# Packing the value projection of a segmented attention kernel, and running its last two blocks as one group

## The chip, the cores and the metric

The kernel runs on one core of a Trainium2 chip. The metric is the device time of one execution in microseconds (us). Engines are named as in the profile: PE is TensorE (matmuls), PEld its weight loads, DVE is VectorE, ACT is ScalarE, POOL is GpSimd, and SP issues most of the DMAs. Line numbers such as L419 are lines of the kernel whose profile is shown.

## The reference

Two branches are added to `x`. Branch B is an MLP mixer, which the change does not touch. Branch A is attention over 64 segments of 32 rows. A segment sees its own rows and some memory rows, which come from the segment before.

```python
# 2048 rows, Dm = 1024, 32 heads of 128, M = 8 memory rows, segments of 32 rows
for s in range(n_seg):
    h = concat([mem, xs])                       # 8 memory rows + 32 rows of the segment
    q, k, v = h @ Wq, h @ Wk, h @ Wv            # each 1024 -> 32 x 128
    p = softmax(mask(q k^T * scale))
    o = (p v) @ Wo
    mem = o[:M]; outs.append(o[M:])
return x + concat(outs) + B(layernorm(x))
```

## The kernel before

The recurrence would run the segments one after another. The kernel guesses all memory rows first (`speculate`), computes all segments in parallel and verifies the guess at the end; a fallback exists and does not run here. The guess gives the eight memory rows that a later segment sees the same value, so one row stands for all eight (the mask adds log2 of 8 to its score), and such a segment takes 33 columns of the transposed activations `hT`. Three segments make a tile of 99 columns (106 for the first, 33 for the last), and four tiles make a block. There are six blocks, and the last one has only two tiles. The weights of a head group (four heads) are three tiles of 1 MB, loaded anew in each block.

```python
for b in range(6):
    hTb = hpool.tile([P, KT, NBMAX], BF16, tag="hTb")       # 403, 396 or 132 columns used
    nc.sync.dma_start(hTb[:, :, lb:nb], hT_d[:, :, c0 + lb:c1])
    ...                                  # DVE writes the guessed memory columns (reps) into hTb
    for hg in range(8):
        wq, wk, wv = ...                 # three loads of 1 MB on SP, four buffers
        for hh in range(4):              # Q; the same for K
            ps = apsum.tile([P, 512], F32, tag="mm")        # two PSUM buffers
            for k in range(KT):
                nc.tensor.matmul(ps[:, :nb], wq[:, k, hh*P:(hh+1)*P], hTb[:, k, :nb], ...)
            nc.scalar.mul(QT[:, hh, :nb], ps[:, :nb], QSCALE)
        for ti, (tok, T, msk) in enumerate(btiles):         # V, one matmul group per tile
            ps = apsum.tile([P, 512], F32, tag="mm")
            for k in range(KT):
                nc.tensor.matmul(ps[:T, :], hTb[:, k, l0:l0+T], wv[:, k, :], ...)
            nc.scalar.copy(V[:T, ti, :], ps[:T, :])
        for ti, (tok, T, msk) in enumerate(btiles):         # attention
            ...  # S = QT^T KT (psS); softmax on DVE and ACT: sm, mx, sm, e, ss, rs, Pn
            ...  # transposes (psT), PT; O = V^T PT (psO), oS on ACT
        ...      # DVE sorts oS into oX (rows) and oT_m (memory rows)
    out_proj(oX, b, ns, mid=(verify() if b == 5 else None))
```

The order of instructions on each engine is fixed when the program is built. Each engine, and SP as the issuer of DMAs, then works through its own list in that order and waits where data or a buffer is missing (below, DVE stands 8.47 us at one such place, with other work behind it).

Of the kernel before, what the change touches and what calls it, by code (L numbers as in the profile page):

```python
# [13 lines left out]
BF16 = mybir.dt.bfloat16  # L14
# [7 lines left out]
P = 128  # L22
# [40 lines left out]
def kernel(  # L63
# [30 lines left out]
    hT_d = tc.dram_tile([P, KT, TH], BF16, name="hT_scratch")  # L94

# [19 lines left out]
    mask40 = const_tile("c_mask40", np.tile(_seg_mask(1, True), (1, 8)))  # L115
    G = cpool.tile([NQ, D], F32)
    ZT = cpool.tile([P, KT, NQ], BF16)
    M0T = cpool.tile([P, KT, M], BF16)
# [10 lines left out]
    def speculate(psum, wpool, spool):  # L129
# [5 lines left out]
        nc.vector.tensor_copy(M0T[:], ps9[:, :, 0:M])  # L135
# [26 lines left out]
        for k0 in (0, 4):  # L162
            ps = psum.tile([P, 4, NQ], F32, tag="tr")
            for k in range(4):
                nc.tensor.matmul(ps[:, k, :], Gb[:, (k0 + k) * P:(k0 + k + 1) * P], ident[:NQ, :NQ], start=True, stop=True)
            nc.vector.tensor_copy(ZT[:, k0:k0 + 4, :], ps[:])
        nc.vector.tensor_reduce(gthr[:], G[:], axis=AX.X, op=ALU.max, apply_absolute_value=True)
        nc.vector.tensor_scalar(gthr[:], gthr[:], TOL, None, op0=ALU.mult)


    actx = ctx.enter_context(ExitStack())
    with ExitStack() as bctx:
# [117 lines left out]
        with ExitStack() as p3:  # L290
# [7 lines left out]
            for tb in range(4):  # L298
# [5 lines left out]
                if tb == 3:  # L304
                    rctx.close()
                    wpool = actx.enter_context(tc.tile_pool(name="aw", bufs=4, side="right"))
                    spool = actx.enter_context(tc.tile_pool(name="aspec", bufs=1, side="right"))
                    hpool = actx.enter_context(tc.tile_pool(name="ah", bufs=2, side="right"))
                    qkv = actx.enter_context(tc.tile_pool(name="aqkv", bufs=2, side="right"))
                    speculate(psum, wpool, spool)  # L310
# [17 lines left out]
    if True:  # L328
# [7 lines left out]
        def out_proj(oX, b, ns, mid=None):  # L336
            for gl in range(ns // 4):
                Gi = 3 * b + gl
                Rt = iop.tile([P, D], F32, tag="Rt")
                nc.sync.dma_start(Rt[:], R_v[:, Gi, :])  # L340
                ot = iop.tile([P, D], BF16, tag="ot")
                for ch in range(2):
                    ps = apsum.tile([P, 512], F32, tag="mm")
                    for h in range(H):
                        nc.tensor.matmul(ps[:], oX[:, h, gl * P:(gl + 1) * P], wo_sb[:, h, ch * 512:(ch + 1) * 512], start=(h == 0), stop=(h == H - 1))  # L345
                    if DEBUG_A:
                        nc.vector.tensor_copy(ot[:, ch * 512:(ch + 1) * 512], ps[:])
                    else:
                        nc.vector.tensor_tensor(ot[:, ch * 512:(ch + 1) * 512], ps[:], Rt[:, ch * 512:(ch + 1) * 512], op=ALU.add)
                    if mid is not None and ch == 0:  # L350
                        mid()
                nc.sync.dma_start(out_v[:, Gi, :], ot[:])

        def verify():
            Dm = iop.tile([NQ, D], F32, tag="Rt")
            for ch in range(2):
                ps = apsum.tile([P, 512], F32, tag="mm")
                for h in range(H):
                    nc.tensor.matmul(ps[:NQ, :], oT_m[:, h, :], wo_sb[:, h, ch * 512:(ch + 1) * 512], start=(h == 0), stop=(h == H - 1))
                nc.vector.tensor_tensor(Dm[:, ch * 512:(ch + 1) * 512], ps[:NQ, :], G[:, ch * 512:(ch + 1) * 512], op=ALU.subtract)  # L360
            dmax = smp.tile([NQ, 1], F32, tag="dmax")
            nc.vector.tensor_reduce(dmax[:], Dm[:], axis=AX.X, op=ALU.max, apply_absolute_value=True)
# [5 lines left out]
            def count():  # L368
                psc = apsum.tile([P, 512], F32, tag="mm")
# [4 lines left out]
        for b in range(6):  # L374
# [8 lines left out]
            if b == 0:  # L383
                nc.vector.tensor_copy(reps[:, :, 1:ns], ZT[:, :, 7:6 + ns])
                nc.vector.tensor_copy(hTb[:, :, 0:M], M0T[:])
            else:
                nc.vector.tensor_copy(reps, ZT[:, :, 12 * b + 6:12 * b + 6 + ns])
            oX = abig.tile([P, H, 384], BF16, tag="oX")
            btiles = tiles[4 * b:4 * b + 4]
            for hg in range(8):  # L390
                cs_ = slice(hg * 512, (hg + 1) * 512)
                hs_ = slice(hg * 4, (hg + 1) * 4)
# [6 lines left out]
                if b == 0 and 1 <= hg < 5:  # L399
                    nc.sync.dma_start(wo_sb[:, (hg - 1) * 8:hg * 8, :], Wo_v[:, (hg - 1) * 8:hg * 8, :])  # L400
                QT = qkv.tile([P, 4, NBMAX], BF16, tag="QT")
                KTt = qkv.tile([P, 4, NBMAX], BF16, tag="KT")
                V = qkv.tile([P, 4, 512], BF16, tag="V")
                oS = qkv.tile([P, 4, NBMAX], BF16, tag="oS")
                for hh in range(4):
                    ps = apsum.tile([P, 512], F32, tag="mm")
                    for k in range(KT):
                        nc.tensor.matmul(ps[:, :nb], wq[:, k, hh * P:(hh + 1) * P], hTb[:, k, :nb], start=(k == 0), stop=(k == KT - 1))  # L408
                    nc.scalar.mul(QT[:, hh, :nb], ps[:, :nb], QSCALE)  # L409
                for hh in range(4):  # L410
                    ps = apsum.tile([P, 512], F32, tag="mm")
                    for k in range(KT):
                        nc.tensor.matmul(ps[:, :nb], wk[:, k, hh * P:(hh + 1) * P], hTb[:, k, :nb], start=(k == 0), stop=(k == KT - 1))  # L413
                    nc.scalar.copy(KTt[:, hh, :nb], ps[:, :nb])  # L414
                for ti, (tok, T, msk) in enumerate(btiles):
                    l0 = tok - c0
                    ps = apsum.tile([P, 512], F32, tag="mm")
                    for k in range(KT):
                        nc.tensor.matmul(ps[:T, :], hTb[:, k, l0:l0 + T], wv[:, k, :], start=(k == 0), stop=(k == KT - 1))  # L419
                    nc.scalar.copy(V[:T, ti, :], ps[:T, :])  # L420
                for ti, (tok, T, msk) in enumerate(btiles):
                    l0 = tok - c0
                    psS = apsum.tile([P, 512], F32, tag="S", bufs=2)
                    S3 = psS[:T, :4 * T].rearrange("p (h k) -> p h k", h=4)
                    for hh in range(4):
                        nc.tensor.matmul(S3[:, hh, :], QT[:, hh, l0:l0 + T], KTt[:, hh, l0:l0 + T], start=True, stop=True)  # L426
                    sm = smp.tile([P, 4, 106], F32, tag="sm")
                    nc.vector.tensor_tensor(sm[:T, :, :T], S3, msk[:].unsqueeze(1).to_broadcast((T, 4, T)), op=ALU.add)  # L428
                    mx = smp.tile([P, 4], F32, tag="mx")
                    nc.vector.tensor_reduce(mx[:T, :], sm[:T, :, :T], axis=AX.X, op=ALU.max)  # L430
                    nc.vector.tensor_tensor(sm[:T, :, :T], sm[:T, :, :T], mx[:T, :].unsqueeze(2).to_broadcast((T, 4, T)), op=ALU.subtract)  # L431
                    e = smp.tile([P, 4, 106], F32, tag="e")
                    nc.scalar.activation(e[:T, :, :T], sm[:T, :, :T], ACTF.Exp, scale=LN2)  # L433
                    ss = smp.tile([P, 4], F32, tag="ss")
                    nc.vector.tensor_reduce(ss[:T, :], e[:T, :, :T], axis=AX.X, op=ALU.add)  # L435
                    rs = smp.tile([P, 4], F32, tag="rs")
                    nc.vector.reciprocal(rs[:T, :], ss[:T, :])  # L437
                    Pn = smp.tile([P, 4, 106], BF16, tag="Pn")
                    nc.vector.tensor_tensor(Pn[:T, :, :T], e[:T, :, :T], rs[:T, :].unsqueeze(2).to_broadcast((T, 4, T)), op=ALU.mult)  # L439
                    psT = apsum.tile([P, 512], F32, tag="T", bufs=1)  # L440
                    T3 = psT[:T, :4 * T].rearrange("p (h k) -> p h k", h=4)
                    for hh in range(4):
                        nc.tensor.matmul(T3[:, hh, :], Pn[:T, hh, :T], ident[:T, :T], start=True, stop=True)  # L443
                    PT = smp.tile([P, 4, 106], BF16, tag="PT")
                    nc.scalar.copy(PT[:T, :, :T], T3)  # L445
                    psO = apsum.tile([P, 512], F32, tag="O", bufs=2)
                    O3 = psO[:, :4 * T].rearrange("p (h k) -> p h k", h=4)
                    for hh in range(4):
                        nc.tensor.matmul(O3[:, hh, :], V[:T, ti, hh * P:(hh + 1) * P], PT[:T, hh, :T], start=True, stop=True)  # L449
                    nc.scalar.copy(oS[:, :, l0:l0 + T], O3)  # L450
                o4 = oS[:, :, lb:lb + 33 * ns].rearrange("p h (j i) -> p h j i", i=33)
                nc.vector.tensor_copy(oX[:, hs_, 0:32 * ns].rearrange("p h (j i) -> p h j i", i=32), o4[:, :, :, 1:33])  # L452
                nc.vector.tensor_copy(oT_m[:, hs_, 7 + 12 * b:7 + 12 * b + ns], o4[:, :, :, 0])
                if b == 0:
                    nc.vector.tensor_copy(oT_m[:, hs_, 0:7], oS[:, :, 0:7])
            out_proj(oX, b, ns, mid=(verify() if b == 5 else None))
# [3 lines left out]
    with tc.If(cond > 0):  # L460
        with ExitStack() as fctx:
# [5 lines left out]
            nc.sync.dma_start(wo_sb[:], Wo_v)  # L467
            hseg = fbig.tile([P, KT, L], BF16)
# [112 lines left out]
```

## Time and profile before

| | before |
|---|---|
| time | 1754.67 us median of 4 runs |
| PE busy | 97% of the span |
| attention part (block 0 to the end) | 586 to 1754.5 us |
| head group of blocks 1 to 4 | 21.1 us |
| head group of block 5 (scores to scores in the timeline) | 9.79 us |

Here are lines of the page of the kernel before: the span, busy time by engine (with share and instruction count), the granted clock in 40 slices (9 is full), and the groups of V (L419) and K (L413; Q, in L408, is like it). A group has busy time and mean ns of one instruction after the bar, then PE's idle time in front of it.

```profile
span 1754.5 us, 25780 instructions
PE 1707.1 (97%) x10705; PEld 923.9 (53%) x10705; DVE 642.4 (37%) x1515; ACT 669.0 (38%) x1347; POOL 90.9 (5%) x117
...
PEclk9999999999999999999999999999999999999999
...
L419 PE MATMUL ps<-wv,hTb 128*99 128x512 bf16 (+2 forms) x1408 | 315.4, 379 | 0.0
L413 PE MATMUL ps<-hTb,wk 128*128 128x396 bf16 (+2 forms) x1536 | 264.8, 313 | 1.7 <-ACT QT L409 1.7
```

PE is nearly always busy and hardly waits. A record of a V matmul lasts 379 ns, but the matmuls start 216 ns apart, so the records overlap. The real pace is read from the chain of the work that ended last (start, us, engine, output, line, count). These lines of it are from block 2:

```profile
1008.65 5.37 PE ps L408 x32
1014.03 5.37 PE ps L413 x32
1019.40 6.91 PE ps L419 x32
...
1040.51 6.91 PE ps L419 x32
```

A group of 32 V matmuls takes 6.91 us, 216 ns each, and the next V group starts 21.11 us later. So V is a third of a head group. It costs that much although its stationary operand has only 99 of 128 columns.

The windows view gives busy time by engine in each stretch, then clock, DMA share and GB/s. The stretches are block 0, block 2, block 5 and the tail.

```profile
core 0: us, PE busy (x) PEld busy (x) DVE busy (x) ACT busy (x) POOL busy (x), PEclk, DMA share, GB/s
586.14:797.44 211.30, 210.05 (x1345) 118.85 (x1345) 94.54 (x222) 94.17 (x193) 0.53 (x1) 1.00 0.54 179
1008.65:1219.67 211.02, 209.06 (x1346) 118.49 (x1344) 93.52 (x215) 92.24 (x192) 0.00 (x0) 1.00 0.43 135
...
1641.68:1718.82 77.14, 74.94 (x818) 51.31 (x816) 29.82 (x100) 39.49 (x122) 0.00 (x0) 1.00 0.89 283
1718.82:1754.50 35.68, 29.34 (x148) 14.00 (x145) 8.39 (x22) 2.33 (x7) 0.00 (x0) 0.97 0.03 9
```

Block 5 stands out with a DMA share of 0.89: it loads the same 24 MB of weights as any block and has a third of the work.

### The profile page before, as it was taken

What the parts mean: (1) busy time and instruction counts of PE and PEld (TensorE: products, weight loads), DVE (VectorE), ACT (ScalarE), POOL (GpSimd) and SP (SyncE); (2) the same over time, 40 slices, a digit from 0 to 9 for tenths busy, and PEclk for the clock granted to TensorE, in tenths of its full rate; (3) what the DMA queues carried; (4) which work ended last, traced back from release to release, by engine and by line L of the source; (5) the groups of instructions that cost most, each with busy time, mean ns of one, the idle gap of its engine ahead of it and who ended that gap; (6) DMA issues with size and microseconds to landing.
All of it is one profiled execution on the core that took longest, in us unless ns stands there. A gap on an engine that the chain in (4) does not pass through costs nothing.

```text
span 1754.5 us, 25780 instructions
## 1 busy us (share of the span) xinstructions
PE 1707.1 (97%) x10705; PEld 923.9 (53%) x10705; DVE 642.4 (37%) x1515; ACT 669.0 (38%) x1347; POOL 90.9 (5%) x117
## 2 busy tenths in 40 slices
PE   5999999999999999999999999999999999999998
PEld 3544444444445555545555455554555555555564
DVE  7447010000002255532555335551455505554242
ACT  6635302021120255513555145551555415553251
POOL 4222010110101000000000000000000000000000
PEclk9999999999999999999999999999999999999999
DMA  9454421121239874434444254451444434443590
GB/s 370 188 171 166 168 84 37 60 61 31 90 116 374 290 261 149 145 103 135 148 145 146 77 162 145 145 163 65 158 144 148 123 102 145 147 155 101 175 328 10
DMA packets 200793, 260.07 MB, mean 148 GB/s; under 512 B 6541, under 2 KB 167352, under 8 KB 200672
## 3 DMA queue, kind: packets, MB, share of 16 engines
q1 hardware_dynamic: 193472, 232.95, 41.3%
q0 software_dynamic: 7200, 25.44, 3.7%
q8 instruction: 85, 1.39, 0.3%
q14 instruction: 36, 0.29, 0.0%
HBM read 228.87 MB, written 29.49 MB: 147 GB/s over the span
## 4 chain that ended last, share of the span: by engine, by line
PE 77%; DVE 8%; ACT 5%; DMA 5%; issue 3%; POOL 0%; SPq 0%; DVEq 0%; ACTq 0%; POOLq 0%
PE ps L419 17%; PE ps L302 11%; PE ps L345 10%; PE ps L322 10%; PE ps L413 9%; PE ps L408 8%; PE psT L443 3%; PE psO L449 2%; PE psS L426 2%; DVE Pn L439 2%; DVE ss L435 2%; ACT e L433 2%; DMA xn_scratch<-xn 1%; DMA wv<-in_A_Wv_dram 1%; DMA hTb<-hT_scratch 1%
## 5 line engine op out<-in xcount | busy, mean ns | idle before, releaser
L419 PE MATMUL ps<-wv,hTb 128*99 128x512 bf16 (+2 forms) x1408 | 315.4, 379 | 0.0
L413 PE MATMUL ps<-hTb,wk 128*128 128x396 bf16 (+2 forms) x1536 | 264.8, 313 | 1.7 <-ACT QT L409 1.7
L408 PE MATMUL ps<-hTb,wq 128*128 128x396 bf16 (+2 forms) x1536 | 261.7, 314 | 1.8 <-DVE Ro L323 0.8
L419 PEld LDWEIGHTS <-hTb 128*99 128x99 bf16 (+2 forms) x1408 | 173.2, 124 | 124.6 <-issue 3.2
L345 PE MATMUL ps<-wo_sb,oX 128*128 128x512 bf16 x1024 | 229.6, 379 | 0.7 <-DVE flag_i L371 0.7
L409 ACT ACTIVATE QT<-ps 128x396 bf16<-128x396 f32 (+2 forms) x192 | 88.8, 463 | 346.2 <-PE ps L408 345.4
L322 PE MATMUL ps<-w_sb,h3T 128*128 128x512 bf16 x896 | 197.1, 379 | 0.0
L302 PE MATMUL ps<-xn3T,w_sb 128*128 128x512 bf16 x896 | 194.4, 379 | 0.0
L428 DVE TENSOR_TENSOR sm<-psS,c_mask_reg_sb 99x396 f32<-99x396 f32 x160 | 87.5, 564 | 290.6 <-PE psS L426 290.6
L420 ACT CAST V<-ps 99x512 bf16<-99x512 f32 (+2 forms) x176 | 103.1, 586 | 202.7 <-PE ps L419 202.7
L408 PEld LDWEIGHTS <-wq 128*128 128x128 bf16 x1536 | 133.8, 98 | 73.5 <-issue 2.4
L413 PEld LDWEIGHTS <-wk 128*128 128x128 bf16 x1536 | 133.3, 98 | 71.2 <-issue 2.6
L303 ACT ACTIVATE h3T<-ps 128x512 bf16<-128x512 f32 x112 | 66.7, 597 | 268.2 <-PE ps L302 268.2
L345 PEld LDWEIGHTS <-oX 128*128 128x128 bf16 x1024 | 97.7, 98 | 111.7 <-DVE oX L452 1.9
L302 PEld LDWEIGHTS <-w_sb 128*128 128x128 bf16 x896 | 87.6, 98 | 105.2
L322 PEld LDWEIGHTS <-h3T 128*128 128x128 bf16 x896 | 86.9, 98 | 103.0
L323 DVE TENSOR_TENSOR Ro<-ps,R 128x512 f32<-128x512 f32 x32 | 22.1, 691 | 296.5 <-PE ps L322 296.4
L445 ACT CAST PT<-psT 99x396 bf16<-99x396 f32 (+2 forms) x176 | 86.2, 490 | 59.2 <-PE psT L443 51.5
L414 ACT CAST KTt<-ps 128x396 bf16<-128x396 f32 (+2 forms) x192 | 87.5, 456 | 53.8 <-PE ps L413 52.5
L435 DVE TENSOR_REDUCE ss<-e 99x4 f32<-99x396 f32 (+2 forms) x176 | 94.7, 546 | 19.4 <-ACT e L433 19.3
L439 DVE TENSOR_TENSOR Pn<-e,rs 99x396 bf16<-99x396 f32 (+2 forms) x176 | 97.5, 558 | 8.1 <-DVE rs L437 0.5
L433 ACT ACTIVATE e<-sm 99x396 f32<-99x396 f32 (+2 forms) x176 | 90.1, 530 | 18.7 <-DVE sm L431 12.7
(101 smaller groups left out, 1317.1 us busy)
## 6 DMA issues: line engine op xcount, KB each, us to landing
wv<-in_A_Wv_dram SPq DMA_DIRECT2D x56, 1024.0 KB, 5.5
wq<-in_A_Wq_dram SPq DMA_DIRECT2D x48, 1024.0 KB, 5.5
wk<-in_A_Wk_dram SPq DMA_DIRECT2D x48, 1024.0 KB, 5.5
xt<-in_A_x_dram SPq DMA_DIRECT2D x32, 256.0 KB, 3.1
R_scratch<-x POOLq DMA_DIRECT2D x16, 512.0 KB, 3.8
R<-R_scratch SPq DMA_DIRECT2D x16, 512.0 KB, 4.1
R_scratch<-Ro POOLq DMA_DIRECT2D x16, 512.0 KB, 5.0
wo<-in_A_Wo_dram SPq DMA_DIRECT2D x8, 1024.0 KB, 9.4
```

Source lines behind the costliest of these rows:

```text
L302: nc.tensor.matmul(ps[:], w3_sb[:, k, f * P:(f + 1) * P], xn3T[:, k, tb * 512:(tb + 1) * 512], start=(k == 0), stop=(k == KT - 1))
L322: nc.tensor.matmul(ps[:], h3T[:, f, j * P:(j + 1) * P], w4_sb[:, f, ch * 512:(ch + 1) * 512], start=(f == 0), stop=(f == FT - 1))
L345: nc.tensor.matmul(ps[:], oX[:, h, gl * P:(gl + 1) * P], wo_sb[:, h, ch * 512:(ch + 1) * 512], start=(h == 0), stop=(h == H - 1))
L408: nc.tensor.matmul(ps[:, :nb], wq[:, k, hh * P:(hh + 1) * P], hTb[:, k, :nb], start=(k == 0), stop=(k == KT - 1))
L409: nc.scalar.mul(QT[:, hh, :nb], ps[:, :nb], QSCALE)
L413: nc.tensor.matmul(ps[:, :nb], wk[:, k, hh * P:(hh + 1) * P], hTb[:, k, :nb], start=(k == 0), stop=(k == KT - 1))
L414: nc.scalar.copy(KTt[:, hh, :nb], ps[:, :nb])
L419: nc.tensor.matmul(ps[:T, :], hTb[:, k, l0:l0 + T], wv[:, k, :], start=(k == 0), stop=(k == KT - 1))
L420: nc.scalar.copy(V[:T, ti, :], ps[:T, :])
L433: nc.scalar.activation(e[:T, :, :T], sm[:T, :, :T], ACTF.Exp, scale=LN2)
L435: nc.vector.tensor_reduce(ss[:T, :], e[:T, :, :T], axis=AX.X, op=ALU.add)
L439: nc.vector.tensor_tensor(Pn[:T, :, :T], e[:T, :, :T], rs[:T, :].unsqueeze(2).to_broadcast((T, 4, T)), op=ALU.mult)
```

## The change

The intent is to project V from tiles of 128 full rows. The 32 real rows of each segment are packed into `xTb`, so 12 segments need three row tiles in place of four. All 71 memory rows are projected once per head group, in block 0, and kept in DRAM. V is still needed in the order of the attention tiles, so small DMAs copy the packed rows, 32 at a time, to their places. Blocks 4 and 5 become one group that loads its weights once. The projections get a third PSUM buffer, `oS` has one buffer, the output projection works on half-width tiles, and its weights `Wo` come in eight loads, one per head group of block 0, in place of four.

```diff
+Vr_d = tc.dram_tile([NQ, H * DH], BF16, name="Vmem_scratch")
-ZT, M0T                                   # memory columns
+MZ = cpool.tile([P, KT, NQ + 1], BF16)    # both in one tile
 ...
+xTb = xvp.tile([P, KT, 32 * ns], BF16, tag="xTb" + sfx, bufs=1)
+nc.vector.tensor_copy(xTb[...], hTb[... columns 1 to 32 of each 33 ...])
 ...
-for ti, (tok, T, msk) in enumerate(btiles):
-    ps = apsum.tile([P, 512], F32, tag="mm")
-    for k in range(KT):
-        nc.tensor.matmul(ps[:T, :], hTb[:, k, l0:l0 + T], wv[:, k, :], ...)
-    nc.scalar.copy(V[:T, ti, :], ps[:T, :])
+for m in range(ns // 4):
+    ps = apsum.tile([P, 512], F32, tag="mm", bufs=3)
+    for k in range(KT):
+        nc.tensor.matmul(ps[:], xTb[:, k, m * P:(m + 1) * P], wv[:, k, :], ...)
+    nc.scalar.copy(Vp[:, m, :], ps[:])
+if b == 0:                                 # the memory rows of all segments
+    for k in range(KT):
+        nc.tensor.matmul(ps[:NQ, :], MZ[:, k, 0:NQ], wv[:, k, :], ...)
+    nc.vector.tensor_copy(vr[:], ps[:NQ, :])
+    nc.gpsimd.dma_start(Vr_d[:, cs_], vr[:])
+for sl in range(ns):                       # 12 copies (4 in block 5)
+    nc.sync.dma_start(V[r0:r0 + SEG, ti, :], Vp[SEG * (sl % 4):SEG * (sl % 4 + 1), sl // 4, :])
+... memory rows: block 0 from vr on POOL, other blocks from Vr_d on SP
 ...
-for b in range(6):
+for group in ((0,), (1,), (2,), (3,), (4, 5)):   # Q of all, K of all, V of all, attention of all
 ... (half-width output tiles, oS with one buffer, Wo in eight loads, a mask loaded in the fallback only: cut)
```

## The prediction

> **What bounds the kernel now.** TensorE. The page has PE busy 97% of the 1754.5 us span, clock row 9 throughout; DVE 37%, ACT 38%. PE's waits add up to some 35 us, mostly in the first stage; under 6 us in the attention blocks (586 us to the end). The timeline of blocks 1 to 4 shows a head group every 21.1 to 21.3 us: 5.37 us each for 32 matmuls of Q and of K (168 ns per 396 columns), 6.91 us for 32 of V (216 ns per 512 columns, from the chain), about 3.6 us for 48 small attention matmuls. The Trainium skill, "TensorE: Matmul & The Clock Gate", section "Back-to-back issue gap", gives N/2.4 + 2.5 ns (216 ns at N=512), without a term for the stationary columns; the trace agrees: V with 99, 106 or 33 stationary columns costs the same (379 to 380 ns records, 216 ns apart).
>
> Block 5 (1642.6 to 1719.0) takes 9.79 us per head group with 3 MB of weights; the windows view shows its DMA near saturation (up to 338 GB/s).
>
> **Removed.** V is projected from rows packed 128 at a time, without memory rows. Blocks 0 to 4: 4 row tiles to 3; block 5: 2 to 1; one extra tile in block 0 does all memory rows. V matmuls go from 1408 to 1088: 320 x 216 ns = 69 us, all on PE's chain: nothing in block 0, 13.8 us in each other block. Fewer evictions on ACT are worth nothing.
>
> **Merging blocks 4 and 5** loads weights once: 24 MB less. Without it block 5 would have become DMA-bound and lost its V gain. Block 5's attention gets more projection work to hide behind: I estimate 7.6 us per head group (2 x 2.1 Q and K, 1.7 V, 1.8 attention) in place of 9.8: 17 us, of which 13.8 is V, so 3 us extra. Tail: about 1 us.
>
> **Added.** 12 copies of 32 KB per head group (4 in block 5) plus the memory rows, SBUF to SBUF, between V's eviction and its use. A DMA issue occupies SP 0.37 us in this trace: about 5 us of SP per 19.5 us. The first use of V (psO) comes 6.6 us after V's last matmul, later tiles by 11 us. Copies may queue behind a 1 MB weight load (5.5 us); that mostly fits. Block 0 adds a serial tail of POOL-issued copies (0.55 us issue each, some 4 us to land), close to 6.6 us. Packing xTb costs DVE a few us per block, hidden. A V tile now depends on several DMAs: more semaphore waits on PE. I charge 0.1 to 0.2 us per head group, up to 1 us in block 0: 5 to 10 us in all. One oS buffer, and both Q/K buffers taken in the merged group, should not stop PE: scores are consumed early.
>
> **Prediction.** 1754.7 - 69 - 4 + 7 = about 1688 us; range 1670 to 1712. Faster by over 2%: 0.93; within 2%: 0.06; slower: 0.01.
>
> **What would show it.** V: 1024 + 64 matmuls, same 379 ns; head group in blocks 1 to 3 about 19.5 us, in block 0 still 21, merged about 27; PE above 95%; weight traffic down 24 MB; small copies landing in 2 to 7 us. Waits of psO on DMA into V under 10 us in total; tens of us would mean late copies.
>
> **What would make it wrong.** V copies stuck behind weight loads, or SP blocked behind a V copy so weights come late; the instruction order placing psO too early; the merged group starved at its last head group; block 0's POOL copies stalling each head group by several us.

## The result, and the profile after

The changed kernel takes 1681.21 us, median of 8 runs (1679.27 to 1683.68), against 1755.83 us for the kernel before in the same rounds. The ratio is 0.9576, with a 95% interval of 0.9566 to 0.9585. A ratio is the mean time of one kernel's fast runs over that of the other's of the same rounds, so it is not quite the ratio of the medians.

These lines of the page after answer to those of before.

```profile
span 1680.2 us, 26399 instructions
PE 1638.0 (97%) x10385; PEld 857.9 (51%) x10385; DVE 650.8 (39%) x1531; ACT 637.6 (38%) x1299; POOL 114.6 (7%) x164
...
L414 PE MATMUL ps<-wv,xTb 128*128 128x512 bf16 x1024 | 227.7, 379 | 0.0
```

The memory rows of block 0 are in a small group, shown by the list of groups by shape:

```profile
L419 PE MATMUL ps<-wv,MZ 128*71 128x512 bf16 x64 | 15.1, 379 | 0.0
```

V went from 1408 to 1024 + 64 matmuls of the same 379 ns, and PE is still 97% busy. By the two pages HBM reads fell from 228.87 to 204.11 MB, as forecast for one block's weights. The chain after, in block 2 and in the merged group (Q and K now share line L402):

```profile
998.36 10.75 PE ps L402 x64
1009.11 5.18 PE ps L414 x24
...
1028.55 5.18 PE ps L414 x24
...
1393.08 14.45 PE ps L402 x128
1407.53 6.91 PE ps L414 x32
...
1434.10 6.91 PE ps L414 x32
```

A head group takes 19.44 us in block 2 (1009.11 to 1028.55); 1.73 us fewer of V would make 19.4. In the merged group the interval between V groups is 26.57 us here and 26.7 us between the later ones (1434.10 to 1460.79). The windows view after, with the same columns, shows block 0, block 2, the merged group and the tail:

```profile
586.83:801.14 214.31, 211.76 (x1345) 112.95 (x1345) 101.19 (x231) 89.98 (x185) 24.83 (x49) 1.00 0.60 191
998.36:1195.58 197.22, 195.82 (x1281) 105.11 (x1280) 94.76 (x216) 87.58 (x184) 0.00 (x0) 1.00 0.52 161
1393.08:1600.95 207.87, 206.11 (x1785) 127.60 (x1783) 105.14 (x281) 113.08 (x285) 0.00 (x0) 1.00 0.40 122
1600.95:1680.20 79.25, 74.28 (x394) 35.23 (x392) 23.71 (x56) 8.20 (x19) 0.00 (x0) 0.98 0.15 46
```

The 74.3 us between the two profiles, by stage:

| stage | before | after | difference | 216 ns x V matmuls |
|---|---|---|---|---|
| before block 0 | 586.14 | 586.83 | +0.7 | 0 |
| block 0 | 211.30 | 214.31 | +3.0 | 0 |
| blocks 1 to 3 | 633.13 | 591.94 | -41.2 | -41.5 |
| blocks 4, 5 and tail | 323.93 | 287.12 | -36.8 | -27.6 |

So in blocks 1 to 3 the copies cost nothing that can be seen, in block 0 something costs 3 us, and the merged end gains 9 us beyond V.

Where are the copies? These lines are from the timeline after, in one head group of block 1 (start, us, engine, line):

```profile
833.71 7.53 SPq L426 DMA_DIRECT2D V<-Vp  x12
...
836.35 0.54 PE L447 MATMUL psS<-KT,QT 128*99 128x99 bf16 x8
...
841.28 0.78 SPq L433 DMA_DIRECT2D V<-Vmem_scratch  x1
...
843.01 0.34 PE L470 MATMUL psO<-PT,V 99*128 99x99 bf16 x4
```

SP needs 7.53 us for the 12 copies; by the view of the tile V a copy occupies SP 588 ns (median). The memory rows go last, at 841.28. The views of this run give no landing time for SP's copies (only 40 small ones by POOL in block 0 have one, 1.8 us). Those of three later runs do: 2.0 to 2.1 us median from issue to landing. With this as an estimate the memory rows arrive at about 843.3, within a few tenths of a us of the first psO at 843.01. PE's list of waits has none for a DMA into V, so they were in time. The copies fit; how little is to spare is asked of a run below.

### The profile page after: what moved, and what is told of

Its sections match the earlier page's. It is cut to its first block, busy times and chain, and to the rows that moved or that the text cites. A ratio compares the mean times of both kernels' runs of the same rounds, so it can differ in the third digit from the quotient of the medians.

```text
span 1680.2 us, 26399 instructions
## 1 busy us (share of the span) xinstructions
PE 1638.0 (97%) x10385; PEld 857.9 (51%) x10385; DVE 650.8 (39%) x1531; ACT 637.6 (38%) x1299; POOL 114.6 (7%) x164
## 3 DMA queue, kind: packets, MB, share of 16 engines
HBM read 204.11 MB, written 30.07 MB: 139 GB/s over the span
## 4 chain that ended last, share of the span: by engine, by line
PE 74%; DVE 12%; ACT 5%; issue 4%; DMA 3%; SPq 1%; POOL 0%; DVEq 0%; ACTq 0%; POOLq 0%
PE ps L402 15%; PE ps L414 13%; PE ps L300 11%; PE ps L345 11%; PE ps L321 11%; PE psT L464 3%; DVE Pn L460 3%; DVE ss L456 2%; PE psO L470 2%; ACT e L454 2%; PE psS L447 2%; DVE sm L449 2%; DVE sm L452 2%; DMA wv<-in_A_Wv_dram 1%; PE ps L245 1%
## 5 line engine op out<-in xcount | busy, mean ns | idle before, releaser
L402 PE MATMUL ps<-hTb,wk 128*128 128x396 bf16 (+2 forms) x1536 | 265.6, 313 | 0.0
L402 PE MATMUL ps<-hTb,wq 128*128 128x396 bf16 (+2 forms) x1536 | 263.5, 314 | 0.8 <-DVE Ro L322 0.8
L414 PE MATMUL ps<-wv,xTb 128*128 128x512 bf16 x1024 | 227.7, 379 | 0.0
L402 PEld LDWEIGHTS <-wq 128*128 128x128 bf16 x1536 | 133.6, 98 | 71.3 <-issue 1.1
L402 PEld LDWEIGHTS <-wk 128*128 128x128 bf16 x1536 | 131.5, 98 | 67.7
L414 PEld LDWEIGHTS <-xTb 128*128 128x128 bf16 x1024 | 99.8, 98 | 115.8
L415 ACT CAST Vp<-ps 128x512 bf16<-128x512 f32 x128 | 74.9, 585 | 151.4 <-PE ps L414 150.3
L466 ACT CAST PT<-psT 99x396 bf16<-99x396 f32 (+1 forms) x176 | 85.9, 488 | 64.0 <-PE psT L464 63.0
L404 ACT CAST KT<-ps 128x396 bf16<-128x396 f32 (+2 forms) x192 | 87.4, 455 | 49.3 <-PE ps L402 49.3
L456 DVE TENSOR_REDUCE ss<-e 99x4 f32<-99x396 f32 (+1 forms) x176 | 95.0, 545 | 22.9 <-ACT e L454 21.9
L460 DVE TENSOR_TENSOR Pn<-e,rs 99x396 bf16<-99x396 f32 (+1 forms) x176 | 97.5, 558 | 7.0
L454 ACT ACTIVATE e<-sm 99x396 f32<-99x396 f32 (+1 forms) x176 | 90.4, 530 | 23.6 <-DVE sm L452 19.7
```

Of the source, the lines that this page charges most:

```text
L402: nc.tensor.matmul(ps[:, :nb], w[:, k, hh * P:(hh + 1) * P], B["hTb"][:, k, :nb], start=(k == 0), stop=(k == KT - 1))
L404: nc.scalar.copy(dst[:, hh, :nb], ps[:, :nb])
L414: nc.tensor.matmul(ps[:], B["xTb"][:, k, m * P:(m + 1) * P], wv[:, k, :], start=(k == 0), stop=(k == KT - 1))
L454: nc.scalar.activation(e[:T, :, :T], sm[:T, :, :T], ACTF.Exp, scale=LN2)
L456: nc.vector.tensor_reduce(ss[:T, :], e[:T, :, :T], axis=AX.X, op=ALU.add)
L460: nc.vector.tensor_tensor(Pn[:T, :, :T], e[:T, :, :T], rs[:T, :].unsqueeze(2).to_broadcast((T, 4, T)), op=ALU.mult)
```

## The experiments

Twelve runs followed. Each is compared with the kernel before in the same rounds (1756.8 to 1757.0 us medians).

| run | time, us | ratio to before |
|---|---|---|
| the changed kernel again | 1682.14 | 0.9570 |
| V unpacked, group merged | 1748.92 | 0.9963 |
| V packed, blocks 4 and 5 apart | 1714.87 | 0.9759 |
| two PSUM buffers in the changed kernel | 1689.63 | 0.9622 |
| three PSUM buffers in the kernel before | 1752.79 | 0.9983 |
| every copy as two, all on SP | 1939.89 | 1.1048 |
| every copy as two, half on POOL | 1682.93 | 0.9579 |
| hTb loads on POOL, memory rows evicted by ACT | 1700.56 | 0.9683 |
| memory columns by POOL, memory rows evicted by ACT | 1678.17 | 0.9555 |
| apart, block 5's copies on POOL | 1723.01 | 0.9815 |
| apart, block 5 without copies (wrong) | 1702.71 | 0.9693 |
| apart, block 5's V unpacked | 1699.58 | 0.9676 |

The changed kernel itself ran again, beside the runs of the copies and of block 0's first mending.

> The changed kernel itself, on the chip of the two runs above, to compare with: 1681 us.

It took 1682.14 us.

### What is packing worth?

```diff
 def proj_V(B, wv, V, cs_):
-    ... packed tiles, memory rows, copies
+    for ti, (tok, T, msk) in enumerate(B["tiles"]):
+        ps = apsum.tile([P, 512], F32, tag="mm", bufs=3)
+        for k in range(KT):
+            nc.tensor.matmul(ps[:T, :], B["hTb"][:, k, l0:l0 + T], wv[:, k, :], ...)
+        nc.scalar.copy(V[:T, ti, :], ps[:T, :])
```

> The changed kernel with V projected the old way (4 row tiles of 99 or 106 rows, 2 in block 5, straight into V, no copies, no xTb); merged group, 3 PSUM buffers and half-width output tiles stay. Theory A: packing is worth its 320 matmuls x 216 ns = 69 us, and the copies cost about 3 us, all in block 0: 1681 + 69 - 3 = 1747 us (1745 to 1749), so merging and the rest are worth about 9 us on the kernel before. Rival B: the copies cost the 7 us of the prediction: 1743 us. Rival C: a part of the 74 us comes from the buffers and tiles, and packing is worth clearly less than 60 us: below 1740 us.

It took 1748.92 us, at the upper edge of theory A and far from rival C. Packing is worth 67.7 us in the merged kernel, 1.4 us short of the full 69.1. The rest of the change is worth 8 us by the medians, or 0.37% by the ratio. About half of it is the third PSUM buffer, which gave the kernel before 4 us by itself (below); the other half is merging together with the half-width tiles, the one `oS` and the pieces of `Wo`, which no run took apart.

### Are the copies free, or just in time?

```diff
-nc.sync.dma_start(V[r0:r0 + SEG, ti, :], Vp[SEG * (sl % 4):SEG * (sl % 4 + 1), sl // 4, :])
+for hf in (0, 16):
+    nc.sync.dma_start(V[r0 + hf:r0 + hf + 16, ti, :], Vp[SEG * (sl % 4) + hf:SEG * (sl % 4) + hf + 16, sl // 4, :])
```

> The changed kernel with each copy of 32 rows of V made as two copies of 16 rows: same bytes, twice the issues. In the changed kernel a copy takes SP 0.59 us, the 12 of a head group 7.5 us, and the memory rows, issued last, are there about when psO first needs them. Theory A (SP's issue time is the scarce thing and there is little slack left): 24 issues take 12 to 15 us, the memory rows come 5 to 7 us late, psO waits on copies for several us in each of 40 head groups: 1720 to 1900 us, unless the scheduler moves psO back and fills the gap, then less. Theory B (copies are far from the critical path): 1681 +- 3 us.

It took 1939.89 us, 258 us more than the changed kernel and 40 us beyond even theory A's range. A copy of 16 rows occupies SP as long as one of 32 rows (587 ns median). The top of PE's list of waits, with total us, number of waits and the longest:

```profile
PE psO L471 <- DMA V<-Vp: 94.2, 53, 3.6
PE ps L402 <- DMA wk<-in_A_Wk_dram: 48.0, 12, 4.4
PE ps L414 <- DMA wv<-in_A_Wv_dram: 25.4, 14, 3.0
```

PE waits for copies (and 18.5 us for memory rows, the next in the list), and also for weights, which stand behind the copies in SP's list. The mean clock fell to 0.942, so a part of the loss is slower matmuls. Does the loss come from SP's issue time and order, or from the number of small copies on the DMA engines? The next run gives the second half of each pair to POOL from block 1 on, and leaves block 0 with single copies:

```diff
-for hf in (0, 16):
-    nc.sync.dma_start(...)
+for hf, eng in ((0, nc.sync), (16, nc.gpsimd)):      # blocks 1 to 5
+    eng.dma_start(...)
```

> As copies_split (two copies of 16 rows for each 32 rows), but from block 1 on the second half of each pair is issued by POOL, and block 0 has the single copies of the changed kernel. Same bytes, same number of small copies as copies_split in blocks 1 to 5; SP issues 12 per head group as in the changed kernel. Theory A (SP's issue time and its order are what made copies_split 258 us slower): 1680 to 1700 us. Theory B (the number of small copies on the DMA engines): 1850 to 1940 us.

It took 1682.93 us. The view of the tile V shows the same number of 16-row copies in blocks 1 to 5, half from each issuer (min/median/max ns):

```profile
L430 SPq DMA_DIRECT2D V<-Vp x416: 507/587/1604, 816.9 to 1610.2; - x139
L430 POOL DMA_DIRECT2D V<-Vp x416: 484/484/1287, 817.2 to 1608.0; - x139
```

So the DMA engines carry twice the copies without harm, and SP's list is the scarce thing. The semaphore updates in the packed traces agree: SP's copies land about as soon after their issue when all are split (median 1.8 us) as in the changed kernel (2.0 us), so nothing was backed up behind the issue. The Trainium skill, "DMA: Bandwidth & Descriptors", section "Issuing engines are not separate DMA queues", says that DMAs of several issuers share the same 16 engines and that issuing from several "will only save the time on the sequencer it takes to initiate the DMA, which is usually small relative to the DMA itself". The first half fits these runs. For copies of 32 KB the second does not: 0.59 us of issue against 2.0 to 2.1 us from issue to landing, and the issues of one list add up.

### Where do block 0's 3 us come from?

In block 0 the head groups take 21.33 us after and 21.02 before, with the same number of V matmuls. DVE evicts the memory rows (0.69 us) ahead of the first softmax step. At the end of the block one more wait shows, in the timeline after:

```profile
759.52 0.65 SPq L383 DMA_DIRECT2D hTb<-hT_scratch  x1
...
767.06 0.38 DVE L389 COPY hTb<-MZ 128x96 bf16<-128x96 bf16 x1 [1.46 <-DMA hTb<-hT_scratch]
...
768.20 0.39 PE L464 MATMUL psT<-c_ident_sb,Pn 99*99 99x99 bf16 x4 [1.42 <-DVE Pn L460]
```

This load of hTb is the one for block 2, since two buffers alternate. SP issues it after the copies, 5.3 us behind the last scores of the block (754.25); in the kernel before it was 0.6 us (752.77 and 752.16). DVE's list has the write of its memory columns amid the softmax of block 0, so DVE stands until it lands and PE waits 1.42 us. A first attempt moved the load to POOL and the eviction to ACT:

```diff
-nc.sync.dma_start(hTb[:, :, lb:nb], hT_d[:, :, c0 + lb:c1])
+nc.gpsimd.dma_start(hTb[:, :, lb:nb], hT_d[:, :, c0 + lb:c1])
-nc.vector.tensor_copy(vr[:], ps[:NQ, :])
+nc.scalar.copy(vr[:], ps[:NQ, :])
```

> The changed kernel with hTb loaded through POOL's queue (in the trace its load for block 1 sat behind 12 copies on SP, 6.8 us later than before, and DVE, waiting for it, kept TensorE waiting 1.4 us) and the memory rows of block 0 evicted by ACT in place of DVE, where the 0.69 us sat ahead of the first softmax step. Theory A (these two make block 0's 3 us): 1678 to 1679.5 us. Rival B (they are noise or come back elsewhere): 1681 +- 0.7 us.

It took 1700.56 us, 19 us slower, so neither theory held for the pair. The eviction on ACT did what it should: most of block 0's head groups took 21.02 us. The load did not. Here is the end of block 2 in the timeline of that run:

```profile
1154.58 0.90 POOL L383 DMA_DIRECT2D hTb<-hT_scratch  x1 [203.19 <-PE ps L402]
...
1162.87 0.38 DVE L389 COPY hTb<-MZ 128x96 bf16<-128x96 bf16 x1 [8.47 <-DMA hTb<-hT_scratch]
...
1164.58 0.50 PE L447 MATMUL psS<-KT,QT 128*99 128x99 bf16 x4 [3.45 <-DVE sm L449]
```

The load started earlier, but the rebuilt list of DVE had the copy that needs it earlier still, and DVE stood for 8.47 us with softmax work behind it. The mistake was to speed up the load of data that DVE need not wait for at all. The second attempt left the load on SP and took the copy out of DVE's list:

```diff
-nc.vector.tensor_copy(reps, MZ[:, :, 12 * b + 7:12 * b + 7 + ns])
+nc.gpsimd.tensor_copy(reps, MZ[:, :, 12 * b + 7:12 * b + 7 + ns])
-nc.vector.tensor_copy(vr[:], ps[:NQ, :])
+nc.scalar.copy(vr[:], ps[:NQ, :])
```

> The changed kernel with two small moves: block 0's memory rows of V are evicted by ACT in place of DVE, and the memory columns of a prefetched hTb are written by POOL in place of DVE (the load itself stays on SP). In the trace of the changed kernel the DVE eviction comes before the first softmax step in each head group of block 0 (21.33 us against 21.02 with ACT in the run htb_pool_vr_act), and DVE waits 8.2 us in all for four loads of hTb that nothing needs yet, which costs TensorE 1.4 us after block 0. Theory A (DVE's queue order is what costs block 0 its 3 us): 1681.2 - 2.2 - 1.4 = 1677 to 1678.5 us. Rival B (it was something else, or POOL brings a new wait): 1680 us or more.

It took 1678.17 us (1677.72 to 1678.58), as theory A said, and it is the fastest of all. Its ratio, 0.9555, lies close to the changed kernel's 0.9570 and 0.9576, with overlapping intervals, so the stage has to decide. Its windows view for block 0:

```profile
584.91:796.05 211.14, 210.22 (x1345) 112.62 (x1345) 95.34 (x222) 94.39 (x193) 25.46 (x50) 1.00 0.61 194
```

Block 0 is back at 211.1 us, so both causes lay in the order of DVE's list.

### Does merging matter, and why?

```diff
-for group in ((0,), (1,), (2,), (3,), (4, 5)):
+for group in ((0,), (1,), (2,), (3,), (4,), (5,)):
```

> The changed kernel, with blocks 4 and 5 as two groups again (V still packed, 3 PSUM buffers for the projections still there). Theory A (of the prediction): alone, block 5 becomes bound by its weight loads. 3 MB per head group at the 338 GB/s seen before is 9.3 us, in place of the 7.24 us that block 5 adds to a merged head group (26.68 - 19.44): +16 us, and about +3 us for the tail: 1698 to 1702 us, with TensorE waiting on loads of weights in block 5. Theory B: block 5 was bound by TensorE all along and merging only removed latency: 9.8 - 1.73 - 0.5 = 7.5 us per head group, total 1684 to 1688 us, no waits on weights.

It took 1714.87 us. This is slower than either theory. The four corners (medians in us) show that the two parts are not additive:

| | blocks 4 and 5 apart | merged |
|---|---|---|
| V as before | 1756.84 (1752.79 with three PSUM buffers) | 1748.92 |
| V packed | 1714.87 | 1681.21 |

Merging is worth 4 us without packing when both sides have three buffers (the half-width tiles and the other small parts of the change counted in), and 34 us with it. The windows view of block 5 in the unmerged run:

```profile
1592.01:1682.52 90.51, 67.75 (x765) 53.42 (x763) 33.60 (x111) 36.91 (x117) 0.00 (x0) 0.91 0.79 245
```

All of PE's waits in that stretch (total us, number, longest):

```profile
PE psT L464 <- DVE Pn L460: 10.0, 7, 2.2
PE ps L414 <- DMA wv<-in_A_Wv_dram: 5.6, 4, 2.0
PE psT L464 <- ACT PT L466: 3.0, 5, 0.6
PE ps L402 <- DMA wk<-in_A_Wk_dram: 2.5, 2, 1.7
PE ps L402 <- DMA wq<-in_A_Wq_dram: 1.2, 1, 1.2
```

Block 5 takes 90.5 us here and took 77.1 us in the kernel before, with 13.8 us more V work. The DMA engines moved 245 GB/s against 283 before. So the loads ran below a rate that they had reached, and PE's waits for weights are not the largest part: they make 9.3 us, softmax 13. SP spent 28.9 us waiting for V's evictions with weight loads behind, so the next run takes the copies of block 5 off SP:

```diff
-nc.sync.dma_start(V[r0:r0 + SEG, ti, :], ...)
+(nc.gpsimd if b == 5 else nc.sync).dma_start(V[r0:r0 + SEG, ti, :], ...)      # and its memory rows
```

> The run unmerged, with the V copies of block 5 alone issued by POOL, so SP only issues weight loads there. Unmerged, block 5 took 11.3 us per head group at 245 GB/s, and SP spent 28.9 us waiting for V's evictions ahead of weight loads. Theory A (the rate of the weight loads sets block 5, SP's order only adds to it): 9.3 to 10 us per head group, near 330 GB/s, total 1700 to 1706 us. Theory B (only SP's order holds it; the loads themselves would keep up with TensorE): about 7.5 us per head group, 1685 to 1689 us. Theory C (neither; a latency chain in block 5): no change, 1713 to 1717 us.

It took 1723.01 us, slower again. None of the three theories had that; C, a latency chain, is nearest. Waits for weights fell to 1.4 us, but psO now waited 16.9 us for copies. These landed 4.8 us (median) after their issue, beside a 1 MB load that SP issued at about the same time or up to 1.4 us earlier. The next run asks what is left when block 5 has no copies at all. Its output is wrong, which doesn't matter for the time. The comparison with the reference still passed, as block 5's share of the output is small against its tolerance.

```diff
 # block 5 only, blocks 4 and 5 apart
-nc.tensor.matmul(O3[:, hh, :], V[:T, ti, ...], PT[:T, hh, :T], ...)
+nc.tensor.matmul(O3[:, hh, :], Vp[:T, 0, ...], PT[:T, hh, :T], ...)     # wrong rows, no copies
-TOL = 2.0 ** -7
+TOL = 2.0 ** 20
```

> Wrong on purpose in block 5: the run unmerged, but block 5's psO reads the packed V (Vp) directly, with matmuls of the same shape, and block 5 makes no copies at all; the failure threshold is raised so that the fallback does not run. It asks whether block 5 alone is held by the rate of its weight loads or by the copies. Theory A (of the prediction; weight loads at about 330 to 338 GB/s): 9.3 to 9.5 us per head group, total 1697 to 1703 us. Theory B (the copies hold it: their latency behind a 1 MB load, and SP's order): 7.3 to 8 us per head group, total 1683 to 1691 us, DMA share near 1.

It took 1702.71 us. The total falls into theory A's range, but by another route than A's. The windows view of its block 5:

```profile
1590.44:1675.84 85.40, 72.16 (x776) 54.93 (x781) 34.19 (x111) 36.58 (x119) 0.00 (x0) 0.86 0.78 248
```

The largest of PE's waits there; the next is 1.3 us for one load of wv:

```profile
PE psT L466 <- DVE Pn L462: 9.8, 8, 1.8
```

Block 5 took 85.4 us, or 10.7 us per head group in place of A's 9.3 to 9.5, at 248 GB/s in place of 330. (This execution was the slowest of the four, 1707.37 us, so its block 5 may be some us longer than usual.) PE hardly waited for weights. It waited 9.8 us for the end of softmax (Pn), and the clock averaged 0.86 with no wait longer than 1.8 us. The timeline of one head group shows why softmax is not covered:

```profile
1625.90 0.92 PE L449 MATMUL psS<-KT,QT 128*99 128x99 bf16 x8
...
1626.75 1.90 PE L414 MATMUL ps<-wv,xTb 128*128 128x512 bf16 x7
...
1628.49 0.51 PE L402 MATMUL ps<-hTb,wq 128*128 128x132 bf16 x6
...
1630.81 0.39 PE L466 MATMUL psT<-c_ident_sb,Pn 99*99 99x99 bf16 x4 [1.81 <-DVE Pn L462]
```

From the scores to their transposes softmax takes 4.9 us, and PE's list has about 2.1 us of work in between (8 matmuls of V at 216 ns, one of which the trace lacks, and 6 of Q at 58 ns). In the last of these runs block 5 is apart with its V projected the old way:

```diff
 def proj_V(B, wv, V, cs_):
+    if b == 5:
+        ... two row tiles straight into V, as in the kernel before
+        return
```

> The run unmerged, with V of block 5 alone projected the old way (two row tiles straight into V, no copies). before_mm3 showed block 5 at 9.6 us per head group with this work. If the copies are what makes block 5 take 11.3 us when packed and alone: 9.6 us per head group, total 1700 to 1704 us, faster than unmerged although TensorE has 13.8 us more work. If something else in the new structure holds block 5: near 1715 us.

It took 1699.58 us, 15 us faster than with block 5 packed and apart, although PE had 13.8 us more to do. The windows view of its block 5:

```profile
1588.84:1666.92 78.08, 76.18 (x840) 52.47 (x838) 33.69 (x111) 41.42 (x127) 0.00 (x0) 1.00 0.86 272
```

The expectation would read this as the copies' fault, but the run without copies does not allow that for the whole: dropping them gained 12 us (1714.87 to 1702.71), and with V unpacked the kernel is 3 us faster still. PE's list there has 60 matmuls of Q and K between scores and transposes, some 3.5 us at 58 ns, and the wait is 0.26 us.

For block 5 packed and apart, waits plus the time lost to the clock add up within 4 us. The sum is rough, since the clock's share is taken of the waiting time too. The work at full pace is an estimate of 57.9 us: 8 head groups of 7.24 us, the difference of 26.68 and 19.44.

| block 5, packed and apart | measured | waits of PE | clock loss, (1 - clock) x time | work + both |
|---|---|---|---|---|
| copies on SP | 90.5 | 22.3 | 8.1 | 88.3 |
| copies on POOL | 102.4 | 27.4 | 18.4 | 103.7 |
| no copies | 85.4 | 12.1 | 12.0 | 82.0 |

That the order of PE's list costs the part that remains without copies is argued from these traces, not shown: no run changed the order alone. What stays open is why the lists were built with so little between scores and transposes in this one arrangement. Also open is how block 5 would run packed, apart and in a better order. By an estimate it would need 3 MB per 7.24 us, over 400 GB/s, while the DMA view of block 5 before has no slice above 375, so the weight rate would then become a limit; none of these runs came to it.

### Does the third PSUM buffer matter?

```diff
 # in the changed kernel
-ps = apsum.tile([P, 512], F32, tag="mm", bufs=3)
+ps = apsum.tile([P, 512], F32, tag="mm", bufs=2)
```

> The changed kernel with 2 PSUM buffers for the projections, as before, in place of 3. Theory A: the third buffer lets the 132-column Q and K groups of block 5 run back to back (57.8 ns per matmul after, about 65 before, with PE waiting for ACT to empty a buffer): 64 x 7 ns x 8 = 3.6 us lost, 1684 to 1686 us, the loss in the merged group, head groups of blocks 1 to 3 still 19.4 us. Rival B: the third buffer is worth nothing: 1681 +- 0.7 us.

```diff
 # in the kernel before, attention part
-ps = apsum.tile([P, 512], F32, tag="mm")
+ps = apsum.tile([P, 512], F32, tag="mm", bufs=3)
```

> The kernel before with 3 PSUM buffers for the projections of the attention part and nothing else changed. It asks what held block 5 at 9.79 us per head group. Theory A (weight loads hold it): still 9.8 us, total 1754 to 1756 us. Theory B (TensorE and its buffer waits hold it): about 9.3 us, total 1750 to 1752 us.

Taking the buffer away cost 8 us (1689.63). The expectation was 3 to 5 us. The windows view of that run, merged group and tail:

```profile
1390.98:1602.50 211.52, 207.64 (x1784) 128.71 (x1783) 105.14 (x281) 115.13 (x285) 0.00 (x0) 1.00 0.39 120
1602.50:1684.90 82.40, 74.53 (x395) 35.59 (x393) 23.70 (x56) 8.20 (x19) 0.00 (x0) 1.00 0.14 44
```

The merged group takes 3.7 us more than in the changed kernel (211.52 and 207.87), which is theory A's part, and the tail 3.2 us more (82.40 and 79.25), which the expectation left out. With three buffers PE starts the output projection between the last softmax steps (1616.57 in the changed kernel); with two it starts it only after them (1623.67), with waits of 0.3 to 0.8 us before. What comes before the merged group happened to be 2.1 us shorter in this profile. Giving the buffer to the kernel before gained 4 us by the medians, with a ratio of 0.9983 (0.9970 to 0.9997): block 5's head group fell from 9.79 to 9.58 us and the tail got shorter. A stage held by its weight loads would not have moved, so this agrees with the section above.

## Why the prediction was right or wrong

The prediction was 1688 us with a range of 1670 to 1712; measured were 1681.2 us. The direction and the main term were right.

- **"320 x 216 ns = 69 us, all on PE's chain: nothing in block 0, 13.8 us in each other block"** was right. Blocks 1 to 3 gained 41.2 of 41.5 us, and packing as a whole is worth 67.7 us in the merged kernel. In these traces a matmul's pace goes with its moving columns (58 ns for 132, 168 for 396, 216 for 512), and filling 128 stationary columns in place of 99 is free: 5.18 us for 24 matmuls with 128 columns is again 216 ns. The Trainium skill, "TensorE: Matmul & The Clock Gate", section "Back-to-back issue gap", gives the formula of the prediction, in the moving columns alone, but for an isolated matmul; for a stream of weight loads and matmuls it gives about 131 ns at 512 columns and says that both set the pace. The measurement decides: this stream ran at 216 ns, so the prediction picked the figure that holds here.
- **"5 to 10 us in all"** for the copies was too large. Blocks 1 to 3 show no loss and block 0 shows 3.0 us. The reason expected for block 0, POOL's serial copies, was not it. It was DVE's list: an eviction ahead of softmax and a wait for a load not yet needed, and moving both gave the 3 us back. The semaphore waits charged at 0.1 to 0.2 us per head group do not show.
- **"A DMA issue occupies SP 0.37 us"** was read from the 1 MB loads; the copies take 0.59 us. The change survived this by luck, since psO came late enough. The prediction thought that this "mostly fits"; it fits without room for twice the issues, as the split copies show.
- **"3 us extra"** and **"Tail: about 1 us"** for merging were undersized: 6.2 us in head groups (8 x (21.11 + 9.79 - 26.68) = 33.8, less 27.6 of V) and 3.0 us in the rest. The term that was mis-sized is Q and K, "2 x 2.1" per head group: it is 3.70 (14.45 - 10.75 in the chain), 58 ns per matmul in place of 65. The run with two PSUM buffers ties 3.7 us in the merged group and 3.2 us in the tail to the third buffer, which the prediction had overlooked. Merging itself was sized well: without packing, and with three buffers on both sides, it brought 3.9 us where 4 were counted.
- **"Without it block 5 would have become DMA-bound and lost its V gain"** had the right outcome and a wrong mechanism. Unmerged, block 5 lost its gain and 13 us more, at a lower DMA rate than before. PE had little work behind softmax, waited for it, for copies and for late weights, and its clock fell to 0.91. The error was to take a high DMA share (0.89) for the limit of a stage in which PE did not wait for any DMA.

Together: block 0 lost 3 us where 7 were charged for the copies, and merging with the third buffer brought 9 us where 4 were counted for merging. Both point the same way, and the kernel came out some 7 us below the forecast.

## What to carry to other kernels

In these traces a matmul costs by its moving columns, whether 33 or 128 stationary ones are filled, so fill them: packing rows is worth what it removes in matmuls, if the rearrangement afterwards stays off the engine that is the bottleneck. When that rearrangement is many small DMAs, add up their issue times on the one engine that issues them, see what stands behind them in its list, and split them over two issuers if it gets tight. A busy share is not a limit: before calling a stage DMA-bound, look for waits on DMAs, and before shrinking a stage's matmul work, ask which latency that work was hiding.

## What the Trainium skill lacked or had wrong

- "DMA: Bandwidth & Descriptors", "Issuing engines are not separate DMA queues", calls the issue time usually small. Here a copy of 16 or 32 rows of 1 KB occupied SP 0.59 us whatever its size (a 1 MB load 0.37 us), against 2.0 to 2.1 us from issue to landing for the 32 rows. Doubling the issues on SP cost 258 us, and giving half of them to POOL (0.48 us each, with block 0 left at single copies) took nearly all of it back.
- "TensorE: Matmul & The Clock Gate", "HAM oscillation — how this bites in real kernels", states the rule as "no PE-idle gaps >~3.4µs". In the run of block 5 without copies the clock averaged 0.86 over 85 us though no single wait of PE was over 1.8 us: the short waits of every head group came with a lower clock. The page's next section, "A second HAM failure mode: psum-queue depth-cycling", tells of another kernel in which short idles did so; what the page lacks is how much idle is enough, and these runs do not show that either. In the trace's clock record the half-clock stretches there last 3.41 or 6.83 us, which agrees with the 3413 ns window of the section "What's actually happening".
- "TensorE: Matmul & The Clock Gate", "Back-to-back issue gap", as said above: about 131 ns per matmul for a stream at 512 columns, where V's groups here ran at 216 ns (6.91 us for 32, 5.18 us for 24); and about 81 ns at 128 columns, where Q and K of block 5 ran at 58 ns with 132.
- No page has it: a prefetch can hold up the engine that touches it. DVE's write into a buffer needed a block later stood in its list amid current work and cost PE 1.4 us (3.45 us where the load was issued by POOL).
